# Moving VectorE's two-stream steps away from GpSimd's sums in a linear-attention and expert-layer kernel

## Chip, cores, metric

The kernel runs on one core of a Trainium2 chip. The metric is device time in microseconds (us) of one execution.

## The reference

Eight batches of linear attention (8 heads, 576 rows, head size 64) feed a layer of four experts over 4608 rows. In short:

```python
def phi(x):
    return np.where(x > 0, x, np.exp(x) - 1.0) + 1.0      # = min(exp(x), max(x + 1, 1))
q_p, k_p = phi(q), phi(k)
kv  = einsum('bhsd,bhse->bhde', k_p, v)
num = einsum('bhsd,bhde->bhse', q_p, kv)
den = einsum('bhsd,bhd->bhs', q_p, k_p.sum(axis=2))[..., None] + 1e-06
x   = num / den                                           # then to rows x 512
p   = domain_probs / (domain_probs.sum(-1, keepdims=True) + 1e-09)
out = sum over e of p[:, e] * (maximum(x @ w1[e], 0) @ w2[e])
```

## The kernel before

Each batch gives a row tile of 512 rows; the 64 rows left over of each batch ("rests") make a ninth tile. From tile 1 on (there, from expert 1 on) the first layer of every expert is a Strassen scheme of seven products per block, and the second layer of experts 0 and 2 is one too. Such a scheme needs sums of blocks: GpSimd forms those of the hidden values, two groups of four per expert.

```python
def hidden_sums(h):                                  # GpSimd, all operands in SBUF
    hs = pm.tile([P, 3, 2, NH], FP16, tag="hs", bufs=2, name="hs")
    ...
    nc.gpsimd.tensor_tensor(out=hs[:, 0], in0=a21, in1=a22, op=AO.add)
    nc.gpsimd.tensor_tensor(out=hs[:, 1], in0=hs[:, 0], in1=a11, op=AO.subtract)
    nc.gpsimd.tensor_tensor(out=a21, in0=a11, in1=a21, op=AO.subtract)
    nc.gpsimd.tensor_tensor(out=hs[:, 2], in0=a12, in1=hs[:, 1], op=AO.subtract)

def p2(self):                                        # one of the seven products
    s2 = self.bank("s")                              # PSUM, two buffers
    self.products(s2, ...)
    add_relu(self.h[:, :, 0, 0:NH], s2, self.u1)     # VectorE; frees the bank
```

While TensorE works on the experts of one tile, the next batch is prepared: ScalarE takes the exponentials (and x+1 of batches 3 to 7), VectorE finishes phi, TensorE forms `kv`.

```python
def phi_dve(self, name, g, part=0, parts=1):         # batches 3..7
    ...
    nc.vector.scalar_tensor_tensor(out=dst, in0=dst, scalar=1.0, in1=ee, op0=AO.max, op1=AO.min)

def left_k(self):                                    # the rests' k, two halves
    ...
    for u in range(2):
        ...
        nc.vector.tensor_scalar(kd, rk[us], 1.0, 1.0, AO.add, AO.max)
        nc.vector.tensor_tensor(out=kd, in0=el[us], in1=kd, op=AO.min)

def kv(self, pair0, n=2):
    ps = aps([P, 2, 2, DE], FP32, "psum_kv")         # the same two "s" banks as p2
    ...
```

Everything is placed by hand in slots, 56 to a tile (a slot is one product, about 0.9 us). A VectorE step of k or q stands two slots behind its ScalarE step. In each tile the hidden sums of expert 0 stand at slots 13 and 20, those of expert 2 at 41 and 48.

```python
dict(v=(-6, -4, -2, 0), k=(6, 8, 10, 12), lv=2, lk=13, kv=(17, 18),
     q=(19, 21, 23, 25), lq=26, qT=28, nd=(38, 40, 41, 43, 45, 46), nl=48),
```

Of the kernel before, what the change touches and what calls it, by code (L numbers as in the profile page):

```python
# [12 lines left out]
AO = mybir.AluOpType  # L13
AF = mybir.ActivationFunctionType
# [6 lines left out]
def kernel(  # L21
# [10 lines left out]
    nc = tc.nc  # L32
# [5 lines left out]
    P = 128  # L38
    HP = P // 2
# [117 lines left out]
    class Batch:  # L157
# [91 lines left out]
            )  # L249

        def left_act(self, *names):
            for name in names:
                i = ("k", "v", "q").index(name)
                el = pa.tile([P, HG * D], FP16, tag="el", bufs=1, name="el")
                nc.scalar.activation(el, self.rl[:, i].rearrange("p h d -> p (h d)"), AF.Exp)
                self.ph["l" + name] = el

        def left_v(self, eng=nc.scalar):
            (eng.copy if eng is nc.scalar else eng.tensor_copy)(
                out=self.vl[:, :, 0:D], in_=self.rl[:, 1]  # L260
            )

        def left_k(self):
            el = self.ph.pop("lk")
            rk = self.rl[:, 0].rearrange("p h d -> p (h d)")
            for u in range(2):
                us = slice(u * HP, (u + 1) * HP)
                kd = self.kl[us, 2 * u : 2 * u + 2].rearrange("p a d -> p (a d)")
                nc.vector.tensor_scalar(kd, rk[us], 1.0, 1.0, AO.add, AO.max)  # L269
                nc.vector.tensor_tensor(out=kd, in0=el[us], in1=kd, op=AO.min)  # L270

        def left_kv(self):
            self.left_act("k")
            self.left_k()
            self.left_v(nc.gpsimd)

        def left_qd(self):
            el = self.ph.pop("lq")
            rq = self.rl[:, 2].rearrange("p h d -> p (h d)")
            qd = self.ql.rearrange("p h d -> p (h d)")  # L280
            nc.vector.tensor_scalar(qd, rq, 1.0, 1.0, AO.add, AO.max)
            nc.vector.tensor_tensor(out=qd, in0=el, in1=qd, op=AO.min)

        def left_q(self):
            self.left_act("q")
            self.left_qd()

        def dma_qT(self):
            nc.sync.dma_start_transpose(
# [395 lines left out]
    def batch_steps(bt, nxt, put, v, k, lv, lk, kv, q, lq, qT, nd, nl):  # L685


        def load(n, g):

            i = QUEUE.index((n, g))  # L690
            n, g = QUEUE[(i + 4) % 6]
            if i < 2:
                bt.load(n, g)
            elif nxt is not None:
                nxt.load(n, g)

        def load_left():
            if nxt is not None:
                nxt.load_left("k", "v", "q")

        def numerators(i0, n):
            bt.nd(i0, n)
            for pair in range(NPAIR):
                if i0 < (pair + 1) * CM <= i0 + n:
                    bt.dma_xT(pair)

        put(min(v[0], k[0]), bt.alloc)
        for i in range(4):
            g, part = divmod(i, 2)
            put(v[i], bt.vcast, g, part, 2)  # L710
            for n, at in (("k", k[i]), ("q", q[i])):
                put(at, bt.phi_act, n, g, part, 2)
                put(at + 2, bt.phi_dve, n, g, part, 2)
                if part:
                    put(at + 4, load, n, g)
            if part:
                put(v[i] + 2, load, "v", g)
        put(lv, bt.left_v)
        put(lk, bt.left_act, "k")
        put(lk + 2, bt.left_k)  # L720
        put(kv[0], bt.kv, 0)
        put(kv[1], bt.kv, 2)
        put(lq, bt.left_act, "q")
        put(lq + 2, bt.left_qd)
        put(lq + 3, load_left)
        put(lq + 4, bt.dma_qTl)
        put(qT, bt.dma_qT)
        for i in range(6):
            put(nd[i], numerators, 3 * i, min(3, NPAIR * CM - 3 * i))
        put(nl, bt.nd_left)  # L730
# [9 lines left out]
    bts = [Batch(b) for b in range(B)]  # L740
    b0, b1 = bts[0], bts[1]
    with tc.manual_schedule(
# [133 lines left out]
        for n, (j, e) in enumerate(units):  # L876
# [11 lines left out]
            else:  # L888
# [3 lines left out]
        SLOTS = (  # L892
            dict(v=(0, 2, 4, 6), k=(1, 3, 5, 7), lv=8, lk=9, kv=(14, 15), q=(16, 17, 19, 20),
                 lq=22, qT=23, nd=(31, 32, 33, 35, 36, 38), nl=40),
            dict(v=(-6, -4, -2, 0), k=(6, 8, 10, 12), lv=2, lk=13, kv=(17, 18),
                 q=(19, 21, 23, 25), lq=26, qT=28, nd=(38, 40, 41, 43, 45, 46), nl=48),
        )
        for j in range(1, NTILES - 1):
            at = 2 * NSLOT * (E * (j - 1) - 1) if j > 1 else 0
            ns = 2 * NSLOT * (E if j > 1 else E - 1)  # L900

            def put(slot, *g):
                work[at + slot].append(g)

            if j == 1:
                put(7, b1.nd_left)
                for i in range(4):
                    put(21 + 3 * i, weight_sums2, 2, i)
            if j + 1 < B:
                nxt = bts[j + 2] if j + 2 < B else None  # L910
                slots = dict(SLOTS[j > 1])
                if j == 2:
                    slots.update(v=(0, 1, 2, 4), lv=5)
                batch_steps(bts[j + 1], nxt, put, **slots)
            for part in range(2):
                put(ns - (6 if j > 1 else 1), token_sums, j + 1, part)

        slot = 0
        for n in range(len(blocks) + 1):
# [47 lines left out]
```

## Time and profile before

| | before |
|---|---|
| time, median of 3 runs | 540.59 us (540.57 to 543.22) |
| TensorE busy in the profiled span of 540.5 us | 506.4 us |
| VectorE, ScalarE, GpSimd busy | 366.2, 284.3, 204.0 us |

First, the kernel's stretches, cut at the same instruction group of each tile (a second-layer group on the chain that ended last). Each line gives the stretch, its length, then the busy time of TensorE, its weight loads, VectorE, ScalarE and GpSimd (with instruction counts), the granted TensorE clock, and the DMA share and rate. The prediction cuts some 5 us later in each tile, so its lengths differ a little.

```profile
core 0: us, PE busy (x) PEld busy (x) DVE busy (x) ACT busy (x) POOL busy (x), PEclk, DMA share, GB/s
141.32:197.54 56.22, 53.46 (x442) 41.39 (x440) 43.95 (x81) 33.62 (x68) 24.03 (x22) 1.00 0.45 113
197.54:255.65 58.11, 55.35 (x442) 41.96 (x440) 44.12 (x81) 33.43 (x67) 23.57 (x22) 0.97 0.37 101
255.65:313.87 58.22, 55.35 (x442) 42.00 (x440) 44.23 (x81) 33.53 (x67) 23.59 (x22) 0.97 0.40 100
...
429.67:480.17 50.50, 50.50 (x401) 39.12 (x400) 29.76 (x53) 22.00 (x40) 22.62 (x20) 1.00 0.06 22
```

The last line has no next batch to prepare: TensorE never stops. The others leave TensorE idle for 2.76 us per tile. The second and third lines also need 1.9 us more of TensorE's busy time for the same 442 matmuls: their granted clock (the share of full speed that TensorE was given) is 0.97 in the mean.

Next, the list of waits: who waited for whom, total us, times, longest.

```profile
PE psum_kv L317 <- DVE h L600: 10.4, 5, 2.1
...
PE py L550 <- ACT acc L459: 1.8, 5, 0.4
PE psum_kv L324 <- DVE kl_63 L270: 1.6, 5, 0.3
```

Five times, once per prepared batch, the second group of `kv` waits 2.1 us for an add-relu of VectorE. The timeline of VectorE and GpSimd shows why (start, us, engine, operation; rows left out are marked):

```profile
203.83 0.74 DVE L461 SCALAR_TENSOR_TENSOR acc<-py,p_sb,acc 128x512 f32<-128x512 f32 x1
203.99 1.15 POOL L524 TENSOR_TENSOR hs<-h 128x512 f16<-128x512 f16 x1 [9.58 <-DVE h L600]
...
204.49 1.20 DVE L235 SCALAR_TENSOR_TENSOR kp<-kp,ee 128x512 f16<-128x512 f16 x1
205.22 1.48 POOL L525 TENSOR_TENSOR hs<-hs,h 128x512 f16<-128x512 f16 x1
205.61 1.24 DVE L269 TENSOR_SCALAR kl_63<-rl 64x256 f16<-64x256 f32 x1
206.67 1.20 POOL L526 TENSOR_TENSOR h<-h 128x512 f16<-128x512 f16 x1
206.95 1.05 DVE L270 TENSOR_TENSOR kl_63<-el,kl_63 64x256 f16<-64x256 f16 x1
207.82 1.20 POOL L527 TENSOR_TENSOR hs<-h,hs 128x512 f16<-128x512 f16 x1
208.04 1.14 DVE L269 TENSOR_SCALAR kl_63<-rl 64x256 f16<-64x256 f32 x1
209.21 0.29 DVE L270 TENSOR_TENSOR kl_63<-el,kl_63 64x256 f16<-64x256 f16 x1
...
210.79 0.68 DVE L600 CUSTOM_DVE_ANT_0 h<-ps,u_2484 128x512 f16<-128x512 f32 x1
...
211.53 0.39 PE L317 MATMUL psum_kv<-vp,kp 128*128 128x130 f16 x4 [2.08 <-DVE h L600]
```

Read it by durations. The same 64x256 step takes 1.05 us beside GpSimd's sums and 0.29 us as soon as GpSimd is done (209.21). Each engine's instruction starts and ends against the other's: VectorE's phi, begun at 204.49, ends at 205.69, half a microsecond after GpSimd's first sum; GpSimd's second sum, begun at 205.22, needs 1.48 us instead of 1.15. That agrees with what the Trainium skill says in "SBUF — State Buffer", section "Who interferes with whom": the two engines share a pair of ports, whoever comes first keeps it for a whole instruction, and a VectorE instruction with two SBUF inputs, or a `tensor_scalar` in a two-port mode, contends with a GpSimd one that reads SBUF. VectorE takes 5.0 us from the phi at 204.49 to the end of the rests' k, and the add-relu that frees the bank for `kv` is late.

Behind this gap TensorE runs slower for some 3.5 us. Four matmuls of one form, before and after it:

```profile
208.41 0.60 PE L616 MATMUL pb<-tt,w_0_72 128*128 128x256 f16 x4
...
213.49 1.06 PE L616 MATMUL pe<-xT,s_0_81 128*128 128x256 f16 x4
```

From 213.5 to 215.2 us the granted clock is 0.50. This is the "half clock" below; it is what makes the mean of the period 0.97.

Over the five tiles, by form (last columns: busy us and mean ns):

```profile
L235 DVE SCALAR_TENSOR_TENSOR qp<-qp,ee 128x512 f16<-128x512 f16 x20 | 17.5, 875 | 0.0
L235 DVE SCALAR_TENSOR_TENSOR kp<-kp,ee 128x512 f16<-128x512 f16 x20 | 15.9, 815 | 0.0
L269 DVE TENSOR_SCALAR kl_63<-rl 64x256 f16<-64x256 f32 x10 | 11.9, 1185 | 0.2
L270 DVE TENSOR_TENSOR kl_63<-el,kl_63 64x256 f16<-64x256 f16 x10 | 6.7, 672 | 0.7
```

### The profile page before, as it was taken

The numbers are of one execution on the slowest core, as the hardware profiler recorded it, in microseconds if no ns is written. First come the engines' busy times: TensorE is split into PE (matmuls) and PEld (weight loads), VectorE is DVE, ScalarE is ACT, GpSimd is POOL, SyncE is SP. The second block draws the span as 40 slices with busy tenths as digits, with TensorE's granted clock in tenths as the row PEclk, the third lists the DMA queues.
The fourth block names the chain that finished last, engine by engine and source line by source line (L and its number), as shares of the span: only waits on it lengthen the run. The fifth ranks groups of instructions, "written<-read, shape, count | busy, mean of one in ns | idle before, by whom it ended". The sixth has DMA issues, their size and how long they took to land.

```text
span 540.5 us, 10008 instructions
## 1 busy us (share of the span) xinstructions
PE 506.4 (94%) x3809; PEld 360.6 (67%) x3809; DVE 366.2 (68%) x691; ACT 284.3 (53%) x548; POOL 204.0 (38%) x207
## 2 busy tenths in 40 slices
PE   6599988999979998999899998999899999999996
PEld 3344444667768775868577866777587878777773
DVE  5434474689777877778866886687768755665573
ACT  5453375862856474836574566547473345335430
POOL 3422223016351634236332824072524550736150
PEclk9899999999999998999989998999899999999999
DMA  9999836563437233533235333522122020001003
GB/s 263 196 208 207 222 99 215 131 179 76 141 106 142 47 100 115 130 74 92 89 111 125 71 115 112 119 47 96 51 53 41 5 79 1 1 21 59 0 2 79
DMA packets 80737, 54.35 MB, mean 101 GB/s; under 512 B 46032, under 2 KB 73680, under 8 KB 80688
## 3 DMA queue, kind: packets, MB, share of 16 engines
q1 hardware_dynamic: 71648, 41.77, 29.3%
q0 software_dynamic: 9040, 11.93, 11.6%
q8 instruction: 30, 0.49, 0.4%
q14 instruction: 19, 0.16, 0.1%
HBM read 45.16 MB, written 9.44 MB: 101 GB/s over the span
## 4 chain that ended last, share of the span: by engine, by line
PE 74%; DVE 13%; ACT 4%; issue 4%; DMA 3%; POOL 0%; ACTq 0%; DVEq 0%
PE py L470 21%; PE pb L616 17%; PE py L550 15%; PE pe L616 8%; PE ph L415 6%; PE ps L616 4%; DVE acc L461 3%; DVE kl_63 L269 2%; DVE h L600 2%; DMA xT<-x_sb 2%; PE psum_nd L357 1%; ACT qp L228 1%; DVE x_sb L340 1%; PE psum_kv L317 1%; DVE kp L235 1%
## 5 line engine op out<-in xcount | busy, mean ns | idle before, releaser
L461 DVE SCALAR_TENSOR_TENSOR acc<-py,p_sb,acc 128x256 f32<-128x256 f32 (+1 forms) x230 | 129.7, 568 | 36.1 <-PE py L550 18.6
L524 POOL TENSOR_TENSOR hs<-h 128x512 f16<-128x512 f16 x30 | 34.6, 1154 | 249.5 <-DVE h L600 249.5
L470 PEld LDWEIGHTS <-h 128*128 128x128 f16 x672 | 66.3, 99 | 30.4
L470 PE MATMUL py<-w_3_79,h 128*128 128x512 f16 x288 | 83.0, 393 | 0.0
L470 PE MATMUL py<-w_1_77,h 128*128 128x512 f16 x288 | 80.6, 379 | 0.0
L660 ACT ACTIVATE h<-pb 128x512 f16<-128x512 f32 x62 | 37.1, 598 | 78.3 <-PE pb L616 78.1
L550 PEld LDWEIGHTS <-h 128*128 128x128 f16 x480 | 46.9, 98 | 6.5 <-issue 0.3
L550 PEld LDWEIGHTS <-hs 128*128 128x128 f16 x360 | 35.2, 98 | 8.4 <-issue 4.0
L525 POOL TENSOR_TENSOR hs<-hs,h 128x512 f16<-128x512 f16 x30 | 38.2, 1274 | 2.3
L459 ACT ACTIVATE acc<-py,p_sb 128x256 f32<-128x256 f32 (+1 forms) x64 | 32.4, 516 | 10.7 <-PE py L470 5.4
L527 POOL TENSOR_TENSOR hs<-h,hs 128x512 f16<-128x512 f16 x30 | 36.7, 1224 | 0.0
L226 ACT ACTIVATE ee<-rawb 128x512 f16<-128x512 f32 (+1 forms) x54 | 36.6, 683 | 0.2
L526 POOL TENSOR_TENSOR h<-h 128x512 f16<-128x512 f16 x30 | 34.9, 1162 | 0.0
L423 ACT ACTIVATE h<-ph 128x512 f16<-128x512 f32 x40 | 23.2, 598 | 21.7 <-PE ph L415 21.5
L616 PEld LDWEIGHTS <-w_1_73 128*128 128x128 f16 x256 | 25.5, 100 | 10.5 <-issue 2.2
L616 PEld LDWEIGHTS <-w_2_74 128*128 128x128 f16 x256 | 24.6, 98 | 9.3
L550 PE MATMUL py<-w_2_78,h 128*128 128x256 f16 x192 | 28.6, 272 | 0.2 <-DVE acc L461 0.2
L616 PEld LDWEIGHTS <-w_3_75 128*128 128x128 f16 x256 | 24.5, 98 | 5.6
L616 PEld LDWEIGHTS <-w_0_72 128*128 128x128 f16 x224 | 21.7, 98 | 8.8
L340 DVE TENSOR_TENSOR x_sb<-psum_nd,recip 128x384 f16<-128x384 f32 (+2 forms) x52 | 25.3, 486 | 2.2 <-POOL hs L527 0.5
L333 ACT CAST kvz_65<-psum_kv 64x130 f16<-64x130 f32 (+1 forms) x36 | 9.0, 251 | 31.7 <-PE psum_kv L324 31.5
L317 PE MATMUL psum_kv<-vp,kp 128*128 128x130 f16 x128 | 11.6, 219 | 14.5 <-DVE h L600 10.4
(529 smaller groups left out, 1063.6 us busy)
## 6 DMA issues: line engine op xcount, KB each, us to landing
out_dram<-acc SPq DMA_DIRECT2D x32, 256.0 KB, 2.4
rawb<-in_v_dram SPq DMA_DIRECT2D x13, 512.0 KB, 4.2
rawb<-in_q_dram SPq DMA_DIRECT2D x13, 512.0 KB, 4.0
rawb<-in_k_dram SPq DMA_DIRECT2D x13, 512.0 KB, 5.1
w_0_72<-in_moe_w_dram POOLq DMA_DIRECT2D x4, 256.0 KB, 6.9
w_0_76<-in_moe_w_dram POOLq DMA_DIRECT2D x2, 512.0 KB, 11.7
w_1_73<-in_moe_w_dram POOLq DMA_DIRECT2D x2, 512.0 KB, 15.1
w_1_77<-in_moe_w_dram POOLq DMA_DIRECT2D x2, 512.0 KB, 18.8
```

The costliest lines, as they stand in the source:

```text
L226: nc.scalar.activation(eeh, src, AF.Exp)
L415: nc.tensor.matmul(out=ph, lhsT=w1_sb[e][:, dc, fj * P : (fj + 1) * P], rhs=xT_of(j)[:, dc], start=(dc == 0), stop=(dc == DC - 1),)
L459: nc.scalar.activation(acc, ps, AF.Identity, scale=pscal)
L461: nc.vector.scalar_tensor_tensor(out=acc, in0=ps, scalar=pscal, in1=acc, op0=AO.mult, op1=AO.add)
L470: nc.tensor.matmul(out=py, lhsT=rows(hT, fj)[:, ns * P : (ns + 1) * P], rhs=w2_sb[e][:, fj, :], start=(fj == 0), stop=(fj == FC - 1),)
L524: nc.gpsimd.tensor_tensor(out=hs[:, 0], in0=a21, in1=a22, op=AO.add)
L525: nc.gpsimd.tensor_tensor(out=hs[:, 1], in0=hs[:, 0], in1=a11, op=AO.subtract)
L526: nc.gpsimd.tensor_tensor(out=a21, in0=a11, in1=a21, op=AO.subtract)
L527: nc.gpsimd.tensor_tensor(out=hs[:, 2], in0=a12, in1=hs[:, 1], op=AO.subtract)
L550: nc.tensor.matmul(out=ps, lhsT=lhsT(k), rhs=rhs[:, k], start=first and k == 0, stop=k == FH - 1, skip_group_check=True,)
L616: nc.tensor.matmul(out=ps[:, kk], lhsT=lk(kc), rhs=rhs[:, kc], start=first and kk == 0 and kc == 0, stop=kc == 1, skip_group_check=True,)
L660: nc.scalar.activation(self.h[:, :, 1, 0:NH], self.b, AF.Relu)
```

## The change

The intent: no VectorE step that reads two SBUF streams should stand where GpSimd is summing. k moves ahead of the first sums (slots 5 to 11), `kv` with it, q behind the second sums (25 to 33). Also, x+1 of the rests goes to ScalarE, so that one VectorE step per part is left. The casts of v move to slots beside the new ones of k. Token sums (GpSimd, for the next tile's first layer) move from slot 50 to 54, and in tile 1 four sums of expert 2's weights (VectorE) move off the hidden sums at 27 and 34.

```diff
         def left_act(self, *names):
...
+                parts = []
+                for u in range(2) if name == "k" else ():
+                    us = slice(u * HP, (u + 1) * HP)
+                    parts.append((us, self.kl[us, 2 * u : 2 * u + 2].rearrange("p a d -> p (a d)")))
+                if name == "q":
+                    parts.append((slice(0, P), self.ql.rearrange("p h d -> p (h d)")))
+                if self.b > 2:
+                    for us, dst in parts:
+                        nc.scalar.activation(dst, src[us], AF.Identity, bias=1.0)
...
-        def left_k(self):
...
+        def left_dve(self, name):
+            src, el, parts = self.ph.pop("l" + name)
+            for us, dst in parts:
+                if self.b > 2:
+                    nc.vector.scalar_tensor_tensor(
+                        out=dst, in0=dst, scalar=1.0, in1=el[us], op0=AO.max, op1=AO.min
+                    )
+                else:
+                    nc.vector.tensor_scalar(dst, src[us], 1.0, 1.0, AO.add, AO.max)
+                    nc.vector.tensor_tensor(out=dst, in0=el[us], in1=dst, op=AO.min)
...
-            dict(v=(-6, -4, -2, 0), k=(6, 8, 10, 12), lv=2, lk=13, kv=(17, 18),
-                 q=(19, 21, 23, 25), lq=26, qT=28, nd=(38, 40, 41, 43, 45, 46), nl=48),
+            dict(v=(0, 1, 2, 4), k=(3, 5, 7, 8), lv=6, lk=9, kv=(14, 16),
+                 q=(23, 25, 27, 29), lq=31, qT=32, nd=(41, 43, 44, 46, 47, 49), nl=50),
...
-                for i in range(4):
-                    put(21 + 3 * i, weight_sums2, 2, i)
+                for i, slot in enumerate((9, 12, 23, 25)):
+                    put(slot, weight_sums2, 2, i)
...
-                put(ns - (6 if j > 1 else 1), token_sums, j + 1, part)
+                put(ns - (2 if j > 1 else 1), token_sums, j + 1, part)
```

## The prediction

> **What bounds it now.** TensorE, busy 506.4 of 540.5 us (page, part 1). From 146.9 us on it is periodic, one period per tile. In the table of stretches the five periods in which a next batch is prepared last 56.4, 58.1, 58.2, 57.9 and 57.8 us; the one without is 50.5 us, TensorE 100% busy. In the first of the five TensorE is busy 53.6 us at full clock, idle 2.76; in the others idle 2.7 to 2.9, granted clock 0.97. So a gapless batch period costs about 53.6 us; the gaps cost 2.8 + 4 x 4.4 = 20 us.
>
> **The gap** (timeline, 204 to 211 us). GpSimd runs four hidden sums while VectorE runs phi of k (1.20 us; 0.67 when GpSimd rests) and the rests' k: 1.24, 1.05, 1.14, 0.29. VectorE falls behind; the add-relu that frees a PSUM bank starts at 210.79, and the second kv group waits 2.08 us for it (list of waits: five times, 10.4 us; 1.6 more for the rests' k). In four of five periods some 3.5 us at half clock follow. The Trainium skill, "SBUF — State Buffer", "Who interferes with whom": a VectorE instruction with two SBUF inputs contends with a GpSimd one that reads SBUF. Durations agree; the second sum stretches too (1.48 against 1.15). "TensorE: Matmul & The Clock Gate", Part 1: idle windows halve the clock; seen after four gaps of five.
>
> **The change.** k's VectorE steps move from slots 8-14 to 5-10, the rests' k from 15 to 11; sums are at 13 and 20, so k is clear of them. q's steps move from 21-27 to 25-31, behind the second sums; kv from 17/18 to 14/16. A slot is about 0.9 us. The rests' four k instructions (3.7 us per period) become two, estimated 0.4 each (a 128x256 three-operand step takes 0.48); q's two become one. phi should take 0.67 throughout (mean now 0.85). VectorE loses about 4 us of 44 per period.
>
> ScalarE gains three Identity steps, about 1.1 us per period, and gets dense: in slots 0-9 casts, k's eight activations and the rests come to 8 us (0.53 each, start to start), with 3 us of other work, against 9: a backlog of 2 to 3 us, bearable because a copy has three slots. In slots 21-35 q (4 x 1.05) meets eight first additions (0.4) and eight copies: TensorE waits 0.36 us per period there now, then 0.3 to 0.7. The rests' k may hold the first kv for up to 0.5. Numerators end 2 to 3 slots later and the token sums move from slot 50 to 54; transposes land in 2.4 us: it should just fit.
>
> Tile 1: weight sums go from slots 21-30 to 9-25, away from the sums at 27 and 34; two took 1.12 and 1.42 us, not 0.6, and TensorE waited 1.14 for a bank. Gain about 1 us.
>
> **Sum.** 540.6 - 20.4 - 1 + about 2.5 of waits that stay or come = 522; range 518 to 530. The gain is idle and half-clock TensorE time: all critical.
>
> **Right if:** kv's wait behind the add-relu is gone; clock 1.00 in all periods; periods 53.6 to 54.5 us; phi 0.6 to 0.7 us; TensorE busy near 499.
>
> **Wrong if:** ScalarE's backlog stalls TensorE over 1 us per period, long enough to halve the clock again; token sums or late transposes hold the next tile's products; or q's steps stay slow.
>
> Chances: faster 0.83, within 2% 0.15, slower 0.02.

## The result

The changed kernel takes 521.94 us (median of 4 runs, 521.05 to 522.74) against 541.9 us (median of 4, 540.57 to 544.26: the three runs above and one more) for the kernel before. The ratio is 0.9627, 95% interval 0.9582 to 0.9671. Ratios here are the mean time of one kernel's runs over that of the other's of the same rounds, so not quite the ratio of the medians. On another chip the unaltered changed kernel gave 521.9 us (6 runs) and 0.9602 (0.9576 to 0.9628).

The stretches after, cut at the same group:

```profile
core 0: us, PE busy (x) PEld busy (x) DVE busy (x) ACT busy (x) POOL busy (x), PEclk, DMA share, GB/s
140.45:194.28 53.83, 53.24 (x441) 41.32 (x440) 39.33 (x78) 34.57 (x72) 22.84 (x22) 1.00 0.39 109
194.28:248.12 53.84, 53.25 (x442) 41.30 (x440) 39.33 (x78) 34.20 (x71) 22.83 (x22) 1.00 0.40 109
248.12:301.97 53.85, 53.27 (x442) 41.32 (x440) 39.34 (x78) 34.21 (x71) 22.83 (x22) 1.00 0.43 108
...
409.65:460.14 50.49, 50.49 (x401) 39.14 (x400) 29.74 (x53) 22.03 (x40) 22.64 (x20) 1.00 0.06 22
```

All five batch tiles now take 53.84 us at full clock, with 0.59 us of idle TensorE. The waits in the same list:

```profile
PE py L556 <- ACT acc L465: 2.7, 5, 0.6
...
PE psum_kv L330 <- DVE kl_63 L283: 0.4, 1, 0.4
```

The wait of `kv` behind an add-relu is gone. What is left per tile is one wait of 0.55 us for a first addition on ScalarE; it was 0.36 before. (The other line is in tile 1.) VectorE and GpSimd around `kv` (its two groups are the PE lines):

```profile
199.26 0.68 DVE L235 SCALAR_TENSOR_TENSOR kp<-kp,ee 128x512 f16<-128x512 f16 x1
199.86 0.86 DVE L278 SCALAR_TENSOR_TENSOR kl_63<-kl_63,el 64x256 f16<-64x256 f16 x2
...
201.49 0.39 PE L323 MATMUL psum_kv<-vp,kp 128*128 128x130 f16 x4
201.52 1.15 POOL L530 TENSOR_TENSOR hs<-h 128x512 f16<-128x512 f16 x1 [10.23 <-DVE h L606]
...
203.80 0.39 PE L323 MATMUL psum_kv<-vp,kp 128*128 128x130 f16 x4
```

k is done at 200.7, the sums start at 201.52, and neither group of `kv` (201.49 and 203.80) waits for anybody. By form:

```profile
L235 DVE SCALAR_TENSOR_TENSOR kp<-kp,ee 128x512 f16<-128x512 f16 x20 | 13.6, 681 | 0.0
L235 DVE SCALAR_TENSOR_TENSOR qp<-qp,ee 128x512 f16<-128x512 f16 x20 | 13.6, 679 | 0.0
L278 DVE SCALAR_TENSOR_TENSOR kl_63<-kl_63,el 64x256 f16<-64x256 f16 x10 | 4.1, 415 | 0.2
```

Where the 20.0 us of span came from, taking the differences of the same cuts in both profiles:

| stretch | before | after | difference |
|---|---|---|---|
| start to the first such cut, in tile 1 | 82.30 | 82.75 | +0.45 |
| from there to the cut in the first batch tile | 59.02 | 57.70 | -1.32 |
| first batch tile | 56.22 | 53.83 | -2.39 |
| four further batch tiles | 232.13 | 215.37 | -16.76 |
| the rest | 110.83 | 110.85 | +0.02 |

The first line varies between 80 and 84 us from profile to profile with the first loads, so differences of a microsecond between whole runs are better read from the periods.

### The profile page after: what moved, and what is told of

It reads as the page before. It is cut to its first block, busy times and chain, and to the rows that moved or that the text cites. A ratio compares the mean times of both kernels' runs of the same rounds, so it can differ in the third digit from the quotient of the medians.

```text
span 520.5 us, 9979 instructions
## 1 busy us (share of the span) xinstructions
PE 498.0 (96%) x3809; PEld 357.7 (69%) x3809; DVE 342.8 (66%) x676; ACT 288.1 (55%) x563; POOL 197.6 (38%) x207
## 4 chain that ended last, share of the span: by engine, by line
PE 81%; ACT 6%; DVE 5%; DMA 5%; issue 2%; POOL 0%; SPq 0%; ACTq 0%; DVEq 0%
PE py L476 26%; PE pb L622 18%; PE py L556 15%; PE pe L622 9%; PE ph L421 5%; PE ps L622 4%; DMA xT<-x_sb 2%; ACT ee L226 2%; DMA rawb<-in_k_dram 2%; PE psum_kv L323 1%; ACT qp L228 1%; DVE acc L467 1%; PE psum_nd L363 1%; DVE x_sb L346 1%; PE warm_ps L742 1%
## 5 line engine op out<-in xcount | busy, mean ns | idle before, releaser
L476 PE MATMUL py<-w_1_77,h 128*128 128x512 f16 x288 | 80.6, 379 | 0.0
L476 PE MATMUL py<-w_3_79,h 128*128 128x512 f16 x288 | 79.3, 379 | 0.0
L531 POOL TENSOR_TENSOR hs<-hs,h 128x512 f16<-128x512 f16 x30 | 34.6, 1155 | 2.4
L533 POOL TENSOR_TENSOR hs<-h,hs 128x512 f16<-128x512 f16 x30 | 34.7, 1156 | 0.0
L622 PEld LDWEIGHTS <-w_2_74 128*128 128x128 f16 x256 | 25.0, 98 | 11.6
L622 PEld LDWEIGHTS <-w_1_73 128*128 128x128 f16 x256 | 24.8, 98 | 7.2
L556 PE MATMUL py<-w_2_78,h 128*128 128x256 f16 x192 | 28.6, 272 | 0.1
L622 PEld LDWEIGHTS <-w_3_75 128*128 128x128 f16 x256 | 24.1, 98 | 5.7
L556 PE MATMUL py<-w_0_76,h 128*128 128x256 f16 x168 | 25.2, 272 | 2.7 <-ACT acc L465 2.7
L622 PEld LDWEIGHTS <-w_0_72 128*128 128x128 f16 x224 | 21.7, 98 | 8.8
L622 PEld LDWEIGHTS <-s_2_83 128*128 128x128 f16 x192 | 18.5, 98 | 7.8
```

The source lines that it names most:

```text
L476: nc.tensor.matmul(out=py, lhsT=rows(hT, fj)[:, ns * P : (ns + 1) * P], rhs=w2_sb[e][:, fj, :], start=(fj == 0), stop=(fj == FC - 1),)
L556: nc.tensor.matmul(out=ps, lhsT=lhsT(k), rhs=rhs[:, k], start=first and k == 0, stop=k == FH - 1, skip_group_check=True,)
L622: nc.tensor.matmul(out=ps[:, kk], lhsT=lk(kc), rhs=rhs[:, kc], start=first and kk == 0 and kc == 0, stop=kc == 1, skip_group_check=True,)
```

## Experiments

Theory 1: VectorE's steps are blocked by GpSimd's sums, so VectorE falls behind just where TensorE needs a bank from it. Theory 2: VectorE simply has too much to do there, and less or differently ordered work is what helps. Theory 3: `kv` stood too early. Four kernels ran on one chip against the kernel before (543.71 us there, 7 runs), four on another (544.26 us, 11 runs), three on a third (544.13 us, 11 runs). All gave correct results.

### The rests' new form alone

The changed kernel, with all places put back to those of before.

> Only the rests' part of the change (Identity on ScalarE, one three-operand step on VectorE), at the old places. Theory 1 (VectorE steps with two SBUF streams are blocked by GpSimd's sums): the two k rests still lie under the sums and take about 1.1 us each instead of 0.43, but they replace four instructions that took 3.9 us start to start, so the add-relu that frees the bank starts about 1.6 us earlier, the wait of the second kv group falls from 2.1 us to about 0.5 and the half clock should go: 525 to 531 us. Theory 2 (what counts is VectorE's amount of work, not the overlap): the rests take 0.43 us each also here and the run takes 521 to 525 us.

Measured: 531.31 us (528.67 to 532.07), ratio 0.9777 (0.9736 to 0.9818). Periods of 55.31 us at full clock. The k rests' new step takes three times its time after the change:

```profile
L278 DVE SCALAR_TENSOR_TENSOR kl<-kl,el 64x256 f16<-64x256 f16 x10 | 13.2, 1318 | 0.2
```

```profile
PE psum_kv L323 <- DVE h L606: 6.8, 5, 1.4
```

So theory 2's durations are refuted: 1.32 us here, 0.415 at the new places, for the same instruction. The wait of `kv` fell only to 1.36 us; I expected about 0.5. The two steps take 2.7 us from start to end where the four took 3.9, so the bank came free 1.2 us earlier and not 1.6; and TensorE, no longer held in the first group of `kv` (0.32 us before), reached the second one some 0.5 us sooner. More than half of the gain came all the same (12.4 us by the medians), mostly because the half clock did not follow a wait of 1.36 us (7.2 us, as priced further below).

### The new places alone

The kernel before with the new slots, token sums and weight sums, and the rests' old four instructions.

> Only the new places (k, kv, q, token sums, weight sums of tile 1), with the rests' old four instructions. Theory 1: out from under the sums the k rests take about 0.3 us each, 1.2 us for the four, phi 0.68; kv's wait is gone and the run takes 521 to 524 us. Theory 2 (amount of VectorE work): VectorE keeps some 0.5 us more per period than in the whole change but 3 us of the old work would stay if the durations did not depend on GpSimd; then a wait of kv of over 1 us stays and the run takes over 530 us.

Measured: 522.11 us (521.29 to 523.01), ratio 0.9599 (0.9564 to 0.9635); periods of 53.85 us against 53.84 with the whole change. The rests' old steps take 0.284 and 0.287 us here:

```profile
L269 DVE TENSOR_SCALAR kl<-rl 64x256 f16<-64x256 f32 x10 | 2.8, 284 | 0.2
```

So the places are the whole gain. The rests' new form saves VectorE 0.5 us per tile at these places (39.33 against 39.82 us busy) and TensorE nothing. From the cut in tile 1 to that in the first batch tile this kernel needs 57.69 us and the one of the experiment above 59.31. There the two differ in the places of the weight sums, and in some first slots of the next tile where neither waits; what went is a wait of 1.1 us for a numerators' bank and smaller ones for VectorE. So the weight sums' places are worth about 1.6 us.

### GpSimd made to wait, VectorE untouched

The kernel before; only the first sums of expert 0 wait for the add-relu that VectorE does behind the rests' k.

```diff
-                def sums(d, hT=hT, hss=hss):
+                def sums(d, hT=hT, hss=hss, late=e == 0):
+                    if late and d == 0:
+                        after = pa.tile([P, 8], FP16, tag="after", bufs=1, name="after")
+                        nc.gpsimd.tensor_copy(out=after, in_=hT[1][:, 0, 1, NH : NH + 8])
                     hss[d] = hidden_sums(hT[d])
...
-                    work[at + (d - 1) * NSLOT].append((sums, d))
+                    work[at + (d - 1) * NSLOT + (3 if e == 0 and d == 0 else 0)].append((sums, d))
```

> The kernel before with VectorE's order untouched; GpSimd's first hidden sums of expert 0 are made to wait, by a small copy that reads it, for the add-relu that VectorE does right behind the k steps. Theory 1: k's phi 0.68 us, the rests' four together about 1.3 us, the wait of the second kv group below 0.3 us, granted clock 1.00; the later sums now collide with q's steps and may hold the first products on hidden sums by up to 1 us per period; 523 to 529 us. Theory 2 (VectorE's work or order as such): kv's wait and the half clock stay, 538 to 542 us.

Measured: 523.06 us (522.74 to 523.15), ratio 0.9616 (0.9582 to 0.9649). The rests' k, GpSimd's late start, and the second group of `kv`, which does not wait:

```profile
203.32 0.29 DVE L269 TENSOR_SCALAR kl<-rl 64x256 f16<-64x256 f32 x1
203.65 0.29 DVE L270 TENSOR_TENSOR kl<-el,kl 64x256 f16<-64x256 f16 x1
...
204.72 0.19 POOL L885 COPY after<-h 128x8 f16<-128x8 f16 x1 [12.75 <-DVE h L600]
...
206.33 0.39 PE L317 MATMUL psum_kv<-vp,kp 128*128 128x130 f16 x4
```

```profile
195.08:248.64 53.56, 53.20 (x441) 41.38 (x440) 41.33 (x81) 33.47 (x67) 23.75 (x23) 1.00 0.39 109
```

This is the experiment that settles it. VectorE has the same instructions in the same order as before, with 1.9 us from the last phi of k to the end of the rests instead of 5.0; it is still busy 2 us more per tile than after the change (41.33 against 39.33 us), and `kv` is at its old place; yet the period is 53.56 us and the wait of `kv` behind the add-relu is gone. Theories 2 and 3 cannot give that. q's phi got slower (1.06 us mean, from 0.875) and no one waited for it. The delayed sums cost 0.4 us each in the last two tiles, where products wait for them. The period is even 0.28 us shorter than after the change: ScalarE's first additions hold TensorE for 0.36 us as before, and not for 0.55. What this kernel loses against the change lies in those last two tiles and in tile 1 (59.44 us against 57.70), where the weight sums are at their old places. The delay together with the weight sums' new places was not run.

### kv two slots later

The kernel before with `kv=(19, 20)`; q's first steps must follow, `q=(21, 22, 23, 25)`, since q takes over k's buffer.

> The kernel before with only kv two slots later (19 and 20 instead of 17 and 18; q's first two steps 21 and 22). The contention stays: k and rests take 1.05 to 1.24 us each. Theory 1 says that this contention costs time only where TensorE has no slack: the wait moves to whatever next needs a bank from VectorE; I expect kv's own wait to fall to 0 to 1 us and the clock to stay full in most periods, 525 to 535 us. Theory 3 (the place of kv alone was wrong): 521 to 524 us. If TensorE waits as long elsewhere: 538 to 542 us.

Measured: 534.19 us (532.86 to 534.75), ratio 0.9818 (0.9781 to 0.9854); periods of 56.0 to 56.3 us at full clock. The wait of `kv` fell to 0.2 us per tile, but others came:

```profile
PE py L550 <- ACT acc L459: 8.2, 15, 1.0
PE pe L616 <- DVE h L600: 2.3, 5, 0.5
...
PE psum_kv L317 <- DVE h L600: 1.1, 5, 0.2
```

ScalarE's q steps, now bunched, delay first additions (8.2 us in all, from 1.8), and VectorE is still late for the next bank. So theory 3 alone is not enough in this layout; but the test is not clean, because q's places had to change with `kv`.

### k put back under the sums

The changed kernel with `k=(8, 10, 12, 13), lk=14, kv=(19, 21)`.

> The changed kernel with k's steps moved back under the first sums (VectorE at 10, 12, 14, 15, the rests at 16; sums start at 13), and kv moved as far behind them as before or further (19 and 21). Theory 1: the last two phi steps and the two rests take 1.0 to 1.2 us each instead of 0.68 and 0.43, about 2.5 us more of VectorE per period; with kv's slack TensorE waits 0 to 1 us per period for it: 522 to 527 us. If the overlap does not matter, the durations stay and the run takes 520 to 522 us.

Measured: 524.94 us (524.03 to 526.8), ratio 0.966 (0.9622 to 0.9697); periods of 54.27 us. k's phi takes 1.05 us in the mean and the rests' step 0.82, VectorE is busy 2.2 us more per tile (41.56 against 39.33), and `kv` waits 0.24 us for the rests' k:

```profile
PE psum_kv L330 <- DVE kl L278: 1.2, 5, 0.2
```

So the overlap comes back in the durations, and costs 0.43 us per tile instead of the 2.8 us of idle time before. Probably this is because `kv` now stands three slots behind the rests' k instead of two and follows in steps of two slots; but the rests' new form, shorter than the old four steps under the sums, is in this kernel too, and the two were not tried apart. That the overlap is dear only together with a near deadline fits this run and is not shown by it alone.

### q put back under the second sums

The changed kernel with `q=(19, 21, 23, 25), lq=26, qT=28`.

> The changed kernel with only q's steps and its transposes at their old places (19 to 25, 26, 28), where VectorE's q steps lie under GpSimd's second sums. Theory 1 with slack: q's phi takes 0.95 to 1.5 us in half of its steps again, but TensorE does not wait for it, since nothing in that stretch needs VectorE soon; periods 53.4 to 54.2 us, 520 to 523 us. If keeping q clear of the sums was needed: 525 us or more.

Measured: 522.05 us (520.51 to 525.26), ratio 0.961 (0.9568 to 0.9652); periods of 53.97 us.

```profile
L235 DVE SCALAR_TENSOR_TENSOR qp<-qp,ee 128x512 f16<-128x512 f16 x20 | 18.4, 921 | 0.0
```

q under the sums is 0.24 us slower per step, and the period 0.13 us longer. Keeping q clear of the sums is nearly worthless for the time; moving k is what counts.

### TensorE kept busy in the gap

The kernel before, with matmuls whose results nobody reads in front of the second `kv` group.

```diff
-            ps = aps([P, 2, 2, DE], FP32, "psum_kv")
+            if self.b > 2 and pair0 == 2:
+                for _ in range(16):
+                    nc.tensor.matmul(
+                        out=self.spare,
+                        lhsT=self.kp[:, 0, 0:2],
+                        rhs=self.vp[:, 0].rearrange("p h d -> p (h d)")[:, 0:248],
+                        start=True,
+                        stop=True,
+                        skip_group_check=True,
+                    )
+            ps = aps([P, 512], FP32, "psum_kv")
+            self.spare = ps[:, 4 * DE : 4 * DE + 248]
+            ps = ps[:, 0 : 4 * DE].rearrange("p (n u d) -> p n u d", n=2, u=2)
```

> The kernel before, with 16 matmuls of 248 columns in front of the second kv group of each later batch, whose results nobody reads (they go to free columns of the first kv group's bank): TensorE works through most of the 2.1 us gap, while the group still starts when VectorE frees its bank. If the half clock after the gap comes of TensorE's idleness, granted clock is 1.00, all five periods take about 56.2 us like the first one now, and the run takes 532 to 535 us. If it comes of something else, four periods stay at 57.9 to 58.2 us and the run takes 540 us or more.

Measured: 535.7 us (534.7 to 536.19), ratio 0.9849 (0.9807 to 0.9891), just past the upper end of what I expected, on a chip where the kernel before took 544.26 us.

```profile
198.33:254.56 56.23, 55.15 (x457) 42.93 (x456) 43.92 (x81) 33.47 (x67) 24.07 (x22) 1.00 0.39 104
```

All five periods are 56.2 us, as the first was before, at full clock. So the half clock comes of the idle gap, and costs 58.03 - 56.23 = 1.8 us in each of four tiles (58.03 is the mean of the four before), 7.2 us in all. The Trainium skill says of the clock gate in "TensorE: Matmul & The Clock Gate", Part 1, that it follows TensorE's recent activity; this run agrees. Useless work at the right place made the kernel 1.5% faster.

### First additions behind product 6 on VectorE

The wait that is left, 0.55 us per tile, is for ScalarE, whose first additions stand behind q's activations. The changed kernel, with two of them moved:

```diff
...
-        if first:
+        if first and vec:
+            nc.vector.tensor_scalar(acc, ps, pscal, None, AO.mult)
+        elif first:
             nc.scalar.activation(acc, ps, AF.Identity, scale=pscal)
...
-        add_acc(j, e, ns, ps, ds, first and e == 0)
+        add_acc(j, e, ns, ps, ds, first and e == 0, p == 6)
```

> The changed kernel, with the two first additions behind product 6 of expert 0 done by VectorE instead of ScalarE. They wait in ScalarE's queue behind q's activations, and TensorE waits 0.55 us per period for the second (2.7 us in all). If ScalarE's queue is the cause, this wait goes, periods become 53.3 us instead of 53.84, and the run takes 518.5 to 520 us. If the wait moves to another first addition or VectorE is late itself: 521 to 523 us.

Measured: 520.84 us (517.7 to 521.38, 6 runs), ratio 0.9569 (0.9537 to 0.9602). The wait left the list and the periods became 53.43 us, a little more than the 53.3 I expected; the whole run is not clearly below the changed kernel's. Three more runs on one chip, to compare without a change of chip:

> The changed kernel once more, unaltered, so that the two that follow are compared with it on one chip: periods 53.84 us, 521 to 523 us.

Measured: 521.9 us (521.09 to 523.68), ratio 0.9602 (0.9576 to 0.9628), periods of 53.84 us.

> The changed kernel with product 6's first additions on VectorE, again: periods 53.43 us, 2 us below the changed kernel of the same chip, 519 to 521 us. If the difference seen before was the chip's, both have the same time.

Measured: 521.02 us (517.64 to 522.56), ratio 0.9573 (0.9541 to 0.9605), at the upper end of what I expected. Here too the period is shorter, TensorE idle 0.04 us in it:

```profile
194.28:247.72 53.44, 53.40 (x442) 41.33 (x440) 40.02 (x80) 33.54 (x69) 22.84 (x22) 1.00 0.40 109
```

> The new places and product 6's first additions on VectorE, but the rests' old four instructions (no Identity of the rests on ScalarE). If the rests' new form is worth nothing at the new places, this takes the time of the one before within 1 us; ScalarE's 1.1 us less per period can then only help. If the new form does save something: 1 to 3 us slower.

Measured: 520.45 us (520.08 to 521.24), ratio 0.9569 (0.9544 to 0.9595), periods of 53.43 us. So the rests' new form is worth nothing here either. By the periods these two are 0.41 x 5 = 2 us faster than the change; by whole runs 0.9 to 1.5 us, with intervals that overlap. The last is the best version that I found, if by little: five of its six runs are below all six of the changed kernel's on the same chip.

## Why the prediction was right

The prediction was 522 us, range 518 to 530; measured 521.94. That the two agree to 0.1 us is luck: I expected a gain of 18.6 us from 540.6, and it was 20.0 us by the medians here, 22.2 on the chip of the repeat, where the kernel before took 544.13 us. Point by point:

- **The gap and its cause.** Right. GpSimd's sums block VectorE's k steps: taking the overlap away at GpSimd's end alone gives 523.06 us with VectorE untouched.
- **20.4 us in the gaps.** About right, in sum and in parts. I took a gapless period to cost 53.6 us; TensorE's busy time per period is 53.25 us after the change, and against that the five periods before (288.35 us) held 22.1 us. Of these 4 x 1.8 = 7.2 us are half clock (I had 1.6 per tile), the rest idle time and its small waits.
- **Waits that stay or come, 2.5 us.** Measured 2.7 us, all of one kind, five times 0.55 us for a first addition on ScalarE behind q's activations; predicted were 0.3 to 0.7 each, and the experiment that moves two of them to VectorE confirms which. TensorE's idle time in the five periods is 5 x 0.59 = 2.95 us, a little more than these waits.
- **The rests' k may hold the first `kv` by up to 0.5 us.** It did not in any batch tile.
- **Tile 1, about 1 us.** 1.32 us between the two profiles; 1.6 us between the two experiments that differ there by the weight sums.
- **Periods of 53.6 to 54.5 us, full clock, phi 0.67, TensorE busy near 499.** 53.84, 1.00, 0.68, 498.0.
- **ScalarE's backlog of 2 to 3 us.** Not measured as such. In the tile shown, VectorE waits twice for a copy of ScalarE near k (1.1 and 1.3 us; once, 1.2 us, before), and TensorE for none.
- **Late numerators and token sums just fit.** TensorE waited for none of them in the batch tiles.
- **What I overrated.** I listed the rests' new form and q's place with the gains, without pricing them apart. The first is worth 0.01 us per tile at the new places, the second 0.13. The expected "VectorE loses about 4 us" was right (4.8 us per tile) and beside the point: VectorE's busy time was not what bound. I also named slow q steps as a sign of being wrong; they come with q's old place and cost next to nothing.

The size came out near because I read it from TensorE's own idle time and clock per period, against a period that had neither, and not from VectorE's savings.

## What to carry to other kernels

When two engines block each other, ask first which of the slowed steps has a near deadline: here only k did, and moving it or delaying the other engine recovered nearly the whole loss. Even under the conflict it cost little with the rests' shorter form and its consumer further off, while q could stay in the conflict at hardly any cost. A gap of TensorE can cost over one and a half times its length (here 2.76 us idle and 1.8 us of half clock) when the clock halves behind it. So price a gap by the whole period against one without it.

## What the Trainium skill lacked or had wrong

- "TensorE: Matmul & The Clock Gate" speaks of idle windows of about 3.4 us. Here waits of 2.1 us (2.08 us in one stretch) halved the clock in four of five tiles of the profile before; waits of 1.36 us in the run with the rests' form alone did so in none of five. How long an idle stretch must be within that range, and why one of five was spared, no run here shows.
- "VectorE: DVE Perf Modes" has no line for `scalar_tensor_tensor` in its table of perf modes. In float16 it takes 0.68 us for 128x512, where `tensor_tensor` takes 0.69 us for 128x1024: half the rate. No page gives its duration; the one line on its rate, in "Vector Engine (DVE) Microarchitecture Reference", section "Points that are easy to get wrong", has no time either. So one fused step (0.415 us for 64x256) saves little against the two that it replaces (0.284 + 0.287 us).
- "SBUF — State Buffer", "Who interferes with whom", agrees with the durations in all runs shown here. It gives no durations for such a pair: beside GpSimd's 1.15 us sums a 64x256 step went from 0.28 to 1.19 us in the mean (`tensor_scalar`) and from 0.415 to 1.32 (`scalar_tensor_tensor`), and GpSimd's second sum from 1.15 to 1.48 us.
